# K one tile ahead of V, P.V one step late, wq in longer runs, and a LayerNorm split around a product, in a memory-bound decode kernel

## The chip, the cores and the metric

The kernel runs on one core of a Trainium2 chip (trn2). The metric is the device time of one execution in microseconds (us). Times quoted below are medians of several executions; the profile's span is one execution, from its first to its last instruction, and is 1.7 to 1.9 us shorter than the time of the same execution.

## The reference, cut to what matters

One decode step (one new token) of a pre-LayerNorm attention block with a key and value cache, followed by a pre-LayerNorm dense block:

```python
B, D, H, Sk, Dh, F = 4, 640, 32, 4096, 128, 1728            # bf16 everywhere
x = A_x                                                     # [4, 1, 640]
q = (layernorm(x) @ wq).reshape(B, 1, H, Dh)
scores = einsum("bhqd,bhkd->bhqk", q, k_cache) * Dh ** -0.5
o = einsum("bhqk,bhkd->bhqd", softmax(scores), v_cache)
h = x + o.reshape(B, 1, H * Dh) @ wo
a = layernorm(h) @ w1 + b1
out = h + (a * tanh(softplus(a))) @ w2
```

The caches are 4 x 32 x 4096 x 128 values each, 134 MB for K and 134 MB for V. Each byte is used once. wq, wo, w1 and w2 together are 15 MB.

## The kernel before: the parts that matter

The caches pass through four SBUF slots of 32 KB per partition ("stream"). A tile is 4 heads of one batch row, 4.19 MB, each partition getting one contiguous row of 32 KB. There are 32 K tiles and 32 V tiles, called k0 to k31 and v0 to v31 here. All loads are issued in order on one queue; a load waits until its slot's former tile has been read.

```python
stream = ctx.enter_context(tc.tile_pool(name="stream", bufs=NSLOT))      # 4 slots

for c in range(DC):                                   # wq: 5 loads of 1 MB, 8 KB runs
    if c % WQC == 0:
        wq_t.append(stream.tile([P, SLOT], BF16, tag="s", name=f"wq{c}"))
    nc.sync.dma_start(out=wq_t[-1][:, (c % WQC) * H * Dh : (c % WQC + 1) * H * Dh],
                      in_=A_wq[c * P : (c + 1) * P, :])
# ...
for i in range(NT - 1):                               # k0 v0 k1 v1 ... k30 k31 v30 v31
    loads.append((load_cache, kt, A_k_cache, i, "k"))
    if i == NT - 2:
        loads.append((load_cache, kt, A_k_cache, NT - 1, "k"))
    loads.append((load_cache, vt, A_v_cache, i, "v"))
loads.append((load_cache, vt, A_v_cache, NT - 1, "v", 4))                # in 4 quarters
loads.append((load_wo_late,))                         # wo (second half), then w1, w2
# ...
loads.append((load_mlp,))
```

For each tile VectorE multiplies K by the query (four multiplies of 2.28 us), TensorE folds the products, VectorE and ScalarE make the exponentials, and TensorE multiplies them with V (P.V).

```python
for i in range(NT):
    issue_loads(i + LA)
    for s in range(NSUB):                             # scores of tile i
        emit_mult(i, s)
        # ... emit_scores, emit_mask, emit_fold
    # ...
    if i < last - 1:
        for s in range(NSUB):
            emit_pv(i, s)                             # P.V of the same tile
        emit_pv_copy(i)
# ... P.V of the last two tiles, wo product into y_ps
```

Behind the attention, LayerNorm is finished before the w1 product starts:

```python
s_ps = ones_d.T @ [y, y*y]                            # (sketch) sums over partitions
# mean, variance, sqrt (ScalarE), reciprocal, (y - mean) * rstd -> ln2 (bf16)
h1_ps = ident.T @ b1T                                 # (sketch) bias first
# 70 matmuls of 4 columns: h1_ps += w1 tile x ln2; exp; mish; 56 matmuls with w2
```

The softmax here doesn't subtract the row's maximum and nothing guards it: scores larger than these inputs give would overflow.

## Time and profile before

| | before |
|---|---|
| median of 3 runs | 676.73 us (676.01 to 677.57) |
| span of the profiled execution | 673.0 us |
| moved | 283.81 MB |
| VectorE / TensorE busy | 61% / 64% |

The first view is from the page of the kernel before: the busy tenths of the 16 DMA engines and what they moved, each in 40 slices of 16.8 us, and the packets.

```profile
DMA  9999999999999999999999999999999999999993
GB/s 368 425 428 434 442 427 422 432 434 439 428 424 432 433 437 428 425 429 435 433 430 428 429 429 435 428 432 433 432 429 430 431 429 433 430 430 433 414 415 160
DMA packets 13015, 283.81 MB, mean 422 GB/s; under 512 B 1652, under 2 KB 1720, under 8 KB 3768
```

The loads never pause.

The second view is the timeline of the end: start, duration, engine, line, operation, output and inputs, and in brackets the idle time and what ended it. `k_3601` is k30, `k_3603` is k31, `v_3705` is v31.

```profile
619.31 4.49 DVE L283 TENSOR_TENSOR prod<-k_3601,qbc 128x4096 bf16<-128x4096 bf16 x2 [5.12 <-DMA k_3601<-in_A_k_cache_dram]
...
634.42 4.49 DVE L283 TENSOR_TENSOR prod<-k_3603,qbc 128x4096 bf16<-128x4096 bf16 x2
...
653.36 1.04 PE L351 MATMUL pv_124<-v_3705,e 128*16 128x512 bf16 x16
...
658.68 0.18 DVE L468 COPY st<-y_ps 128x20 f32<-128x20 f32 x1 [0.87 <-PE y_ps L408]
...
661.22 4.74 PE L522 MATMUL h_ps<-ln_4048,w_slot 128*64 128x4 bf16 x70 [1.39 <-DVE ln_4048 L502]
...
669.84 0.32 DVE L571 CAST o_bf<-y_ps 128x160 bf16<-128x160 f32 x1 [2.24 <-PE y_ps L565]
```

The first multiply of k30 waits for its load, that of k31 does not: it follows k30's. The last P.V, w1 and w2 products wait for no load either. From 619.3 on the end is compute.

The third view is the windows of the same stretch: start and end in us, length, then for PE (TensorE matmuls), PEld (weight loads), DVE (VectorE), ACT (ScalarE) and POOL the busy time and the count of instructions, then the granted TensorE clock (1.00 is full speed), the DMA share and GB/s.

```profile
656.00:658.00 2.00, 2.00 (x80) 2.00 (x80) 0.37 (x2) 0.00 (x0) 0.00 (x0) 0.97 1.03 423
658.00:660.00 2.00, 1.34 (x28) 1.21 (x25) 0.71 (x4) 1.09 (x2) 0.00 (x0) 0.50 1.02 417
660.00:662.00 2.00, 0.78 (x13) 0.76 (x13) 0.79 (x6) 1.92 (x3) 0.00 (x0) 0.50 0.69 282
662.00:664.00 2.00, 2.00 (x34) 1.97 (x33) 0.00 (x0) 0.04 (x1) 0.00 (x0) 0.50 0.47 188
664.00:666.00 2.00, 2.00 (x31) 1.87 (x30) 0.00 (x0) 0.01 (x1) 0.00 (x0) 0.50 0.14 58
```

The loads run at full rate until 660 and fade out until almost 666 (w2 is the last). The granted clock is 0.50 from 658 on.

### The profile page before, as it was taken

The page shows a single profiled execution, that of the slowest core. Times are in us where ns is not written, and L with a number is a line of the kernel's source. Part 1 is how long each engine was busy: PE and PEld are TensorE (multiplying, and loading weights), DVE is VectorE, ACT ScalarE, POOL GpSimd, SP SyncE. Part 2 cuts the span into 40 slices and gives each one's busy share as a digit, 9 for nine tenths or more (in the row PEclk, how much of TensorE's full clock was granted, in tenths as well). Part 3 has the DMA queues.
Part 4 walks back from the last instruction along what each step waited for, and adds up shares of the span by engine and source line. Part 5 has one row for each costly group of instructions (what it writes and reads, how often), then busy time and mean ns, then how long its engine had stood idle before and what let it go on. Part 6 is the DMA issues. An engine that isn't in the chain of part 4 may idle for free.

```text
span 673.0 us, 6966 instructions
## 1 busy us (share of the span) xinstructions
PE 431.2 (64%) x2933; PEld 192.9 (29%) x2933; DVE 410.7 (61%) x474; ACT 75.4 (11%) x312; POOL 1.9 (0%) x9
## 2 busy tenths in 40 slices
PE   1947765755767745776566667476557766655776
PEld 0313322322323312332223323222223322222335
DVE  3455665755658746576555767585565766576842
ACT  0401100111101101010000110011010100001011
POOL 1000000000000000000000000000000000000000
PEclk9979767889868878896687987787788967788895
DMA  9999999999999999999999999999999999999993
GB/s 368 425 428 434 442 427 422 432 434 439 428 424 432 433 437 428 425 429 435 433 430 428 429 429 435 428 432 433 432 429 430 431 429 433 430 430 433 414 415 160
DMA packets 13015, 283.81 MB, mean 422 GB/s; under 512 B 1652, under 2 KB 1720, under 8 KB 3768
## 3 DMA queue, kind: packets, MB, share of 16 engines
q1 hardware_dynamic: 12656, 283.27, 98.3%
q8 instruction: 23, 0.38, 0.2%
q10 hardware_dynamic: 328, 0.09, 0.1%
q14 instruction: 8, 0.07, 0.0%
HBM read 283.35 MB, written 0.01 MB: 421 GB/s over the span
## 4 chain that ended last, share of the span: by engine, by line
DMA 59%; DVE 19%; PE 19%; issue 1%; ACT 0%; SPq 0%; DVEq 0%; ACTq 0%
DVE prod L283 16%; PE red L295 14%; DMA k_342<-in_A_k_cache_dram 4%; DMA k_1516<-in_A_k_cache_dram 4%; DMA k_1041<-in_A_k_cache_dram 4%; DMA k_1991<-in_A_k_cache_dram 4%; DMA k_566<-in_A_k_cache_dram 4%; DMA k_2464<-in_A_k_cache_dram 4%; DMA k_3370<-in_A_k_cache_dram 4%; DMA k_2917<-in_A_k_cache_dram 4%; DMA k_3148<-in_A_k_cache_dram 4%; DMA k_1767<-in_A_k_cache_dram 4%; DMA k_817<-in_A_k_cache_dram 3%; DMA k_2695<-in_A_k_cache_dram 3%; DMA k_3601<-in_A_k_cache_dram 3%; DMA k_1292<-in_A_k_cache_dram 3%
## 5 line engine op out<-in xcount | busy, mean ns | idle before, releaser
L295 PE MATMUL red<-prod,ident 128*128 128x512 bf16 x1024 | 302.3, 454 | 218.7 <-DVE prod L283 217.7
L295 PEld LDWEIGHTS <-ident 128*128 128x128 bf16 x1024 | 116.5, 115 | 386.1 <-issue 319.7
L312 DVE TENSOR_REDUCE s_f<-red 128x32 f32<-128x512 f32 x128 | 88.0, 688 | 79.3 <-PE red L295 79.2
L315 ACT ACTIVATE ex<-s_f 128x32 bf16<-128x32 f32 x128 | 29.4, 229 | 518.0 <-DVE s_f L312 518.0
L322 DVE TENSOR_TENSOR e<-ex,hmask 128x128 bf16<-128x128 bf16 x128 | 36.4, 284 | 6.1 <-ACT ex L315 6.1
L372 PEld LDWEIGHTS o_ps<-selo,pv_sb 128*128 128x128 f32 x256 | 33.4, 191 | 6.0 <-ACT pv_sb L362 1.7
L351 PEld LDWEIGHTS <-e 128*16 128x16 bf16 x1024 | 18.4, 88 | 45.8 <-DVE e L322 21.8
L372 PE MATMUL o_ps<-selo,pv_sb 128*128 128x4 f32 x256 | 30.6, 243 | 0.7 <-ACT pv_sb L362 0.7
L315 ACT ACTIVATION_READ_ACCUMULATOR ex<-s_f 128x1 f32 x128 | 23.8, 186 | 0.0
L283 DVE TENSOR_TENSOR prod<-k_82,qbc 128x4096 bf16<-128x4096 bf16 x4 | 9.1, 2286 | 17.9 <-DMA k_82<-in_A_k_cache_dram 17.9
L378 DVE TENSOR_TENSOR OT<-o_ps,rl 128x16 bf16<-128x16 f32 x8 | 1.6, 195 | 21.7 <-PE o_ps L372 21.7
L255 PE MATMUL q_ps<-wq_74,lnT 128*4 128x512 bf16 x32 | 10.9, 463 | 4.1 <-DMA wq_74<-in_A_wq_dram 4.1
L283 DVE TENSOR_TENSOR prod<-k_244,qbc 128x4096 bf16<-128x4096 bf16 x4 | 9.1, 2286 | 6.7 <-DMA k_244<-in_A_k_cache_dram 6.7
L283 DVE TENSOR_TENSOR prod<-k_1415,qbc 128x4096 bf16<-128x4096 bf16 x4 | 9.1, 2285 | 6.7 <-DMA k_1415<-in_A_k_cache_dram 6.7
L283 DVE TENSOR_TENSOR prod<-k_3148,qbc 128x4096 bf16<-128x4096 bf16 x4 | 9.1, 2285 | 6.3 <-DMA k_3148<-in_A_k_cache_dram 6.3
L283 DVE TENSOR_TENSOR prod<-k_940,qbc 128x4096 bf16<-128x4096 bf16 x4 | 9.1, 2287 | 6.1 <-DMA k_940<-in_A_k_cache_dram 6.1
L283 DVE TENSOR_TENSOR prod<-k_1767,qbc 128x4096 bf16<-128x4096 bf16 x4 | 9.1, 2285 | 5.9 <-DMA k_1767<-in_A_k_cache_dram 5.9
L283 DVE TENSOR_TENSOR prod<-k_1890,qbc 128x4096 bf16<-128x4096 bf16 x4 | 9.1, 2287 | 5.7 <-DMA k_1890<-in_A_k_cache_dram 5.7
L283 DVE TENSOR_TENSOR prod<-k_465,qbc 128x4096 bf16<-128x4096 bf16 x4 | 9.1, 2286 | 5.7 <-DMA k_465<-in_A_k_cache_dram 5.7
L283 DVE TENSOR_TENSOR prod<-k_2363,qbc 128x4096 bf16<-128x4096 bf16 x4 | 9.1, 2285 | 5.6 <-DMA k_2363<-in_A_k_cache_dram 5.6
L283 DVE TENSOR_TENSOR prod<-k_2695,qbc 128x4096 bf16<-128x4096 bf16 x4 | 9.1, 2286 | 5.1 <-DMA k_2695<-in_A_k_cache_dram 5.1
L283 DVE TENSOR_TENSOR prod<-k_3601,qbc 128x4096 bf16<-128x4096 bf16 x4 | 9.1, 2284 | 5.1 <-DMA k_3601<-in_A_k_cache_dram 5.1
(175 smaller groups left out, 377.9 us busy)
## 6 DMA issues: line engine op xcount, KB each, us to landing
wq_74<-in_A_wq_dram SPq DMA_DIRECT2D x4, 1024.0 KB, 9.7
k_82<-in_A_k_cache_dram SPq DMA_DIRECT2D x1, 4096.0 KB, 20.5
v_84<-in_A_v_cache_dram SPq DMA_DIRECT2D x1, 4096.0 KB
k_244<-in_A_k_cache_dram SPq DMA_DIRECT2D x1, 4096.0 KB
v_246<-in_A_v_cache_dram SPq DMA_DIRECT2D x1, 4096.0 KB
k_342<-in_A_k_cache_dram SPq DMA_DIRECT2D x1, 4096.0 KB
v_344<-in_A_v_cache_dram SPq DMA_DIRECT2D x1, 4096.0 KB, 35.1
k_465<-in_A_k_cache_dram SPq DMA_DIRECT2D x1, 4096.0 KB
```

The source lines that it names most:

```text
L255: nc.tensor.matmul(q_ps[:, :], lhsT=lnT[:, c, :], rhs=wq_t[c // WQC][:, o : o + 512], start=(c == 0), stop=(c == DC - 1),)
L283: nc.vector.tensor_tensor(out=t[:, :, :], in0=kt[i][:, s * RS : (s + 1) * RS, :], in1=q_bc[hg][:, b, :].unsqueeze(1).to_broadcast([P, RS, ...
L295: nc.tensor.matmul(red[:, :, :], lhsT=ident[:, :], rhs=t[:, :, c * CW : (c + 1) * CW], start=(c == 0), stop=(c == Dh // CW - 1),)
L312: nc.vector.tensor_reduce(out=s_t[i][:, sl], in_=reds.pop((i, s))[:, :, :], axis=AX.X, op=ALU.add)
L315: nc.scalar.activation(out=ex_t[i][:, sl], in_=s_t[i][:, sl], func=ACT.Exp, scale=SCALE, accum_out=rs_t[hg][:, b, s : s + 1],)
L322: nc.vector.tensor_tensor(out=e_t[i][:, sl, :], in0=ex_t[i][:, sl].unsqueeze(2).to_broadcast([P, RS, G]), in1=hmask[:, :].unsqueeze(1).to_ ...
L351: nc.tensor.matmul(pvs[i % 2][k * QD : k * QD + RQ * G, :], lhsT=e_t[i][:, u * RQ : (u + 1) * RQ, :], rhs=vt[i][:, u * RQ : (u + 1) * RQ, ...
L372: nc.tensor.matmul(o_ps[hg][:, b, :], lhsT=t[:, r, :], rhs=selo[:, r, :], start=(r == 0), stop=(r == RQ - 1),)
L378: nc.vector.tensor_tensor(out=OT[:, hg * G : (hg + 1) * G, :].rearrange("p g b -> p b g"), in0=o_ps.pop(hg)[:, :, :], in1=rl.pop(hg)[:, :] ...
```

## The change

Its intent: let the last K tile arrive before its scores are needed and the last P.V wait for nothing but V; load wq in fewer, longer runs; and start the w1 product as soon as the mean is known, with the square root and 1/std behind it (the bias is multiplied by std so that it comes out right).

```diff
-    for c in range(DC):
-        if c % WQC == 0:
-            wq_t.append(stream.tile([P, SLOT], BF16, tag="s", name=f"wq{c}"))
+    wq_v = A_wq.rearrange("(p c) n -> p (c n)", c=DC)
+    for c0 in range(0, DC, WQC):
+        n = min(WQC, DC - c0) * H * Dh
+        wq_t.append(stream.tile([P, SLOT], BF16, tag="s", name=f"wq{c0}"))
         nc.sync.dma_start(
-            out=wq_t[-1][:, (c % WQC) * H * Dh : (c % WQC + 1) * H * Dh],
-            in_=A_wq[c * P : (c + 1) * P, :],
+            out=wq_t[-1][:, 0:n], in_=wq_v[:, c0 * H * Dh : c0 * H * Dh + n]
         )
# ...
-    for i in range(NT - 1):
+    for i in range(NT):
         loads.append((load_cache, kt, A_k_cache, i, "k"))
-        if i == NT - 2:
-            loads.append((load_cache, kt, A_k_cache, NT - 1, "k"))
-        loads.append((load_cache, vt, A_v_cache, i, "v"))
+        if i > 0:
+            loads.append((load_cache, vt, A_v_cache, i - 1, "v"))
# ... w2_tail's load moves from the head to behind tile 0
+    ident_f = consts.tile([P, P], FP32)
+    nc.vector.tensor_copy(out=ident_f[:, :], in_=ident[:, :])
# ... 
-        if i < last - 1:
+        if i > 0:
             for s in range(NSUB):
-                emit_pv(i, s)
-            emit_pv_copy(i)
+                emit_pv(i - 1, s)
+            emit_pv_copy(i - 1)
# ... w1 product: rhs=ln2 becomes rhs=cen (mean taken off, bf16); the bias follows by
+            nc.tensor.matmul(
+                h1_ps[:, :, :], lhsT=ident_f[:, :], rhs=b1s[:, :, :], start=False, stop=False
+            )
# ... and behind the product
+    h1 = consts.tile([P, FC, N], FP32)
+    nc.vector.tensor_tensor(
+        out=h1[:, :, :], in0=h1_ps[:, :, :],
+        in1=rstd[:, :].unsqueeze(1).to_broadcast([P, FC, N]), op=ALU.mult,
+    )
```

More of the change, by code (lines that the diff above doesn't have):

```diff
@@ L158 @@
     )
-    nc.scalar.dma_start(out=w2_tail[0:FT, :], in_=B_w2[FM * P : F, :])
     ident = consts.tile([P, P], BF16)
@@ L228, with transposed @@
     )
-    def transposed(rows, dst):
+    def transposed(rows, dst, split):
         tp = ps.tile([P, DC * N], FP32, tag="misc", name="tp")
@@ L234, in transposed @@
                 tp[:, c * N : (c + 1) * N],
-                lhsT=rows[0:N, c * P : (c + 1) * P], rhs=ident[0:N, 0:N],
+                lhsT=split(rows)[:, c, :], rhs=ident[0:N, 0:N],
                 start=True, stop=True,
@@ L241 @@
     xT = consts.tile([P, DC, N], BF16)
-    transposed(ln1, lnT[:, :, :])
-    transposed(x_bf, xT[:, :, :])
+    transposed(ln1, lnT[:, :, :], lambda t: t[:, :].rearrange("n (p c) -> n c p", c=DC))
+    transposed(x_bf, xT[:, :, :], lambda t: t[:, :].rearrange("n (c p) -> n c p", c=DC))
     nc.vector.tensor_copy(
@@ L429 @@
             emit_fold(i, s)
-            if i > 0 and s == 1 and i < last:
-                emit_o(i - 1)
-                if b == 0:
+            if i > 1 and s == 1:
+                emit_o(i - 2)
+                if b == 1:
                     emit_ot(hg - 1)
-            if b == 0 and i > 0 and s == 2:
+            if hg > 0 and b == 1 and s == 2:
                 emit_perm(hg - 1)
-            if b == 0 and i > 0 and s == 3 and hg <= WLATE:
+            if hg > 0 and b == 1 and s == 3 and hg <= WLATE:
                 emit_wo(hg - 1)
@@ L440 @@
         emit_mask(i, NSUB - 1)
-        if i < last - 1:
+        if i == 0:
+            nc.scalar.dma_start(out=w2_tail[0:FT, :], in_=B_w2[FM * P : F, :])
+            nc.scalar.dma_start(
+                out=w2_tail[FT : FT + CG, :], in_=B_w2[F - CG : F, :]
+            )
+        if i > 0:
             for s in range(NSUB):
-                emit_pv(i, s)
-            emit_pv_copy(i)
+                emit_pv(i - 1, s)
+            emit_pv_copy(i - 1)
         if b == N - 1:
@@ L448 @@
             emit_qbc(hg + 1)
-    for s in range(NSUB):
-        emit_pv(last - 1, s)
-    emit_pv_copy(last - 1)
     emit_pv(last, 0)
@@ L464 @@
     emit_wo(WLATE + 3)
+    FC = FM + 1
+    h1_ps = ps.tile([P, FC, N], FP32, tag="red", name="h1_ps")
+    nc.tensor.matmul(
+        h1_ps[:, :, :], lhsT=zeros[:, :], rhs=zeros[:, 0 : FC * N], start=True, stop=False
+    )
     st = consts.tile([P, 2, DC, N], FP32)
@@ L469, with emit_mean @@
     nc.scalar.activation(out=st[:, 1, :, :], in_=y_ps[:, :, :], func=ACT.Square)
-    s_ps = ps.tile([P, 2 * DC * N], FP32, tag="misc", name="s_ps")
-    nc.tensor.matmul(
-        s_ps[:, :], lhsT=ones_d[:, :], rhs=st[:, :, :, :].rearrange("p k c n -> p (k c n)"),
-        start=True, stop=True,
-    )
+    s_ps = []
+    for k in range(2):
+        t = ps.tile([P, DC * N], FP32, tag="misc", name="s_ps")
+        nc.tensor.matmul(
+            t[:, :], lhsT=ones_d[:, :], rhs=st[:, k, :, :].rearrange("p c n -> p (c n)"),
+            start=True, stop=True,
+        )
+        s_ps.append(t)
+    mu = consts.tile([P, 2, N], FP32)
+    def emit_mean(k):
+        nc.vector.tensor_reduce(
+            out=mu[:, k, :], in_=s_ps[k][:, :].rearrange("p (c n) -> p n c", c=DC),
+            axis=AX.X, op=ALU.add,
+        )
+    emit_mean(0)
+    cen = consts.tile([P, DC, N], BF16)
+    nc.vector.tensor_tensor(
+        out=cen[:, :, :], in0=st[:, 0, :, :],
+        in1=mu[:, 0, :].unsqueeze(1).to_broadcast([P, DC, N]), op=ALU.subtract,
+    )
+    emit_mean(1)
+    msq = consts.tile([P, N], FP32)
+    nc.vector.tensor_tensor(out=msq[:, :], in0=mu[:, 0, :], in1=mu[:, 0, :], op=ALU.mult)
+    var = consts.tile([P, N], FP32)
+    nc.vector.tensor_tensor(out=var[:, :], in0=mu[:, 1, :], in1=msq[:, :], op=ALU.subtract)
+    std2 = consts.tile([P, N], FP32)
+    nc.scalar.activation(
+        out=std2[:, :], in_=var[:, :], func=ACT.Sqrt, bias=eps4[:, :], scale=1.0
+    )
+    b1s = consts.tile([P, FC, N], FP32)
+    nc.vector.tensor_tensor(
+        out=b1s[:, :, :], in0=b1T[:, :].unsqueeze(2).to_broadcast([P, FC, N]),
+        in1=std2[:, :].unsqueeze(1).to_broadcast([P, FC, N]), op=ALU.mult,
+    )
+    rstd = consts.tile([P, N], FP32)
+    nc.vector.reciprocal(out=rstd[:, :], in_=std2[:, :])
     h_hi = consts.tile([P, DC, N], BF16)
@@ L480 @@
     )
-    mu = consts.tile([P, 2, N], FP32)
-    nc.vector.tensor_reduce(
-        out=mu[:, :, :],
-        in_=s_ps[:, :].rearrange("p (k c n) -> p k n c", k=2, c=DC),
-        axis=AX.X, op=ALU.add,
-    )
-    msq = consts.tile([P, N], FP32)
-    nc.vector.tensor_tensor(out=msq[:, :], in0=mu[:, 0, :], in1=mu[:, 0, :], op=ALU.mult)
-    var = consts.tile([P, N], FP32)
-    nc.vector.tensor_tensor(out=var[:, :], in0=mu[:, 1, :], in1=msq[:, :], op=ALU.subtract)
-    rstd = consts.tile([P, N], FP32)
-    nc.scalar.activation(
-        out=rstd[:, :], in_=var[:, :], func=ACT.Sqrt, bias=eps4[:, :], scale=1.0
-    )
-    cen = consts.tile([P, DC, N], FP32)
-    nc.vector.tensor_tensor(
-        out=cen[:, :, :], in0=st[:, 0, :, :],
-        in1=mu[:, 0, :].unsqueeze(1).to_broadcast([P, DC, N]), op=ALU.subtract,
-    )
-    nc.vector.reciprocal(out=rstd[:, :], in_=rstd[:, :])
-    ln2 = consts.tile([P, DC, N], BF16)
-    nc.vector.tensor_tensor(
-        out=ln2[:, :, :], in0=cen[:, :, :],
-        in1=rstd[:, :].unsqueeze(1).to_broadcast([P, DC, N]), op=ALU.mult,
-    )
-    FC = FM + 1
-    w1_sb = mlp_w["w1"]
-    h1_ps = ps.tile([P, FC, N], FP32, tag="red", name="h1_ps")
-    nc.tensor.matmul(
-        h1_ps[:, :, :], lhsT=ident[:, :],
-        rhs=b1T[:, :].unsqueeze(2).to_broadcast([P, FC, N]), start=True, stop=False,
-    )
+    w1_sb = mlp_w["w1"]
     for c0, c1 in zip(W1S, W1S[1:]):
+        if c1 == DC:
+            nc.tensor.matmul(
+                h1_ps[:, :, :], lhsT=ident_f[:, :], rhs=b1s[:, :, :], start=False, stop=False
+            )
         for j in [FM] + list(range(FM)):
@@ L522 @@
                 nc.tensor.matmul(
-                    h1_ps[0 : (P if j < FM else FT), j, :], lhsT=w, rhs=ln2[:, c, :],
+                    h1_ps[0 : (P if j < FM else FT), j, :], lhsT=w, rhs=cen[:, c, :],
                     start=False, stop=(c == DC - 1 and j == FM - 1),
@@ L546 @@
     hm2 = consts.tile([P, FC, N], FP32)
-    nc.scalar.activation(out=ta[:, :, :], in_=h1_ps[:, :, :], func=ACT.Exp, scale=1.0)
-    nc.vector.tensor_scalar_mul(out=hm2[:, :, :], in0=h1_ps[:, :, :], scalar1=-2.0)
+    h1 = consts.tile([P, FC, N], FP32)
+    nc.vector.tensor_tensor(
+        out=h1[:, :, :], in0=h1_ps[:, :, :],
+        in1=rstd[:, :].unsqueeze(1).to_broadcast([P, FC, N]), op=ALU.mult,
+    )
+    nc.scalar.activation(out=ta[:, :, :], in_=h1[:, :, :], func=ACT.Exp, scale=1.0)
+    nc.vector.tensor_scalar_mul(out=hm2[:, :, :], in0=h1[:, :, :], scalar1=-2.0)
     nc.vector.scalar_tensor_tensor(
```

## The prediction

> **What bounds the kernel now.** The DMA stream. The page shows 283.81 MB moved, DMA 9 in 39 of 40 slices, and 422 to 442 GB/s in slices 2 to 37 (mean about 430). The Trainium skill, "DMA: Bandwidth & Descriptors", "Where 436 GB/s comes from", puts the fabric ceiling at 435 GB/s; this trace agrees with it within about 1%. Reordering cache loads cannot speed the middle. DVE (61%) and PE (64%) finish a tile in about 15 us (k30 landed at 619.3, next multiply at 634.4; timeline) where two cache tiles take 19.4 us to arrive. Only head and tail can move.
>
> **Tail before** (timeline, windows, issue times plus landing times). k30 lands at 619.3 and k31, by my estimate, at 629.2 (4.19 MB at 425 GB/s), but k31's multiply starts at 634.4 because k30 is still being scored: 5.2 us lost. Scores end at 649.0, last P.V at 654.4, wo product 658.7, first w1 matmul 661.2, w1 done 665.9, act at 667.6, w2 done 669.8, end 673.0. Loads meanwhile: the last v quarter about 648.6, w1 660.5, last piece of w2 about 665.6 (issued 651.8, 13.8 us to landing). So compute ends about 2 us behind the last load.
>
> **What the change does.**
> - k30 moves from 61st to 60th cache tile, so it lands near 609.6, and k31 no longer waits behind it: its multiply starts at 629.2 when it lands. Scores end about 644 (-5). P.V of tile 31 then waits for v31 (648.6) and ends about 649.3 (-5).
> - But wo comes behind v31: its last quarter lands about 654.9 (2.62 MB at 415 GB/s), so y is done about 655.5 to 656.3 (-2.5 to -3).
> - The mean alone ahead of w1: before, y to w1 took 2.57 us with a 1.28 us table load, square root and reciprocal in it. After: about 1.5 us (-1). Added: a float32 bias matmul (about 0.3, mostly hidden) and one 128x56 multiply by 1/std (about 0.25) behind w1.
> - w1's 70 matmuls took 4.74 us, 68 ns each, at a granted clock of 0.50 (windows 658 to 672), which I expect to stay. The Trainium skill, "TensorE: Matmul & The Clock Gate", "Part 1", names 4/8 as the cold state; the trace agrees (0.50). They also wait for w1's last piece at 660.1 to 660.5. w1 done about 662 to 663, act about 664.5.
> - w2's last piece still lands about 665.5, unmoved. w2 done 666 to 667.1, output 3.2 us later: 669.3 to 670.4 against 673.0.
>
> **Head.** wq as one 32 KB-run load: its five pieces landed 2.5 us apart (419 GB/s; 430 would save 0.3 us). k0 follows behind (26.2), so 0 to 0.4 us.
>
> **Sum.** -2.6 to -3.7 in the tail, 0 to -0.4 in the head: about -3.3 us, 0.5%. 676.7 becomes 673.4 us; range 670.6 to 676.2. Faster by over 2%: 0.01; within 2%: 0.98; slower: 0.01.
>
> **What would show it.** Slices of the middle unchanged near 430 GB/s; last k multiply about 5 us earlier and released by its own DMA; P.V of the last tile released by DMA v; wo and w1 products with DMA waits; no square root between y and the first w1 matmul.
>
> **What would make it wrong.** A change of the mean DMA rate by 0.5% from the new order is 3 us, as large as the gain. A stall in the load queue (late slot release of v29 or k31). A last w2 landing that moves. The clock falling to 0.50 already during the wo product (gives back about 1.5 us).

## The result, and the profile after

The kernel after took 669.51 us (669.23 to 669.87, 4 runs) against 676.89 us for the kernel before (676.01 to 677.57, 4 runs): 7.4 us less. A ratio is the mean time of one kernel's runs over that of the other's of the same rounds, so it is not quite the ratio of these medians: 0.9892, 95% interval 0.9875 to 0.9909. That is inside 2%, as forecast, but below the stated range of 670.6 to 676.2, and 2.2 times the predicted gain. The two profiled executions differ by less, 673.0 against 667.5 us of span: the profiled one of the kernel before took 674.76 us and was faster than the others of its kernel here.

The page of the kernel after, same lines as before:

```profile
DMA  9999999999999999999999999999999999999995
GB/s 376 440 411 438 419 438 435 432 427 439 432 427 430 430 436 429 438 437 423 432 437 431 433 428 436 437 430 427 434 437 436 429 429 432 438 431 430 427 415 241
DMA packets 12591, 283.81 MB, mean 425 GB/s; under 512 B 1608, under 2 KB 1680, under 8 KB 3728
```

The timeline of the end of the kernel after (`k_3545` is k31, `v_3666` is v31):

```profile
627.02 4.50 DVE L284 TENSOR_TENSOR prod<-k_3545,qbc 128x4096 bf16<-128x4096 bf16 x2 [4.92 <-DMA k_3545<-in_A_k_cache_dram]
...
646.49 0.61 PE L352 MATMUL pv_124<-v_3666,e 128*16 128x512 bf16 x8 [1.04 <-DMA v_3666<-in_A_v_cache_dram]
...
653.39 0.18 DVE L477 COPY st<-y_ps 128x20 f32<-128x20 f32 x1 [2.29 <-PE y_ps L409]
...
656.90 1.89 PE L537 MATMUL h_ps<-cen,w_slot 128*64 128x4 bf16 x28 [0.20 <-DMA w_slot<-in_B_w_dram]
...
664.37 0.33 DVE L591 CAST o_bf<-y_ps 128x160 bf16<-128x160 f32 x1 [2.24 <-PE y_ps L585]
```

And its windows:

```profile
648.00:650.00 2.00, 2.00 (x37) 2.00 (x38) 0.19 (x1) 0.00 (x0) 0.00 (x0) 0.56 1.02 420
...
656.00:658.00 2.00, 1.80 (x29) 1.70 (x29) 0.09 (x1) 0.78 (x1) 0.00 (x0) 0.50 1.01 407
658.00:660.00 2.00, 2.00 (x27) 1.88 (x27) 0.00 (x0) 0.00 (x0) 0.00 (x0) 0.50 0.70 291
660.00:662.00 2.00, 1.12 (x23) 0.63 (x21) 1.41 (x6) 0.25 (x1) 0.00 (x0) 0.50 0.47 196
662.00:664.00 2.00, 1.82 (x56) 1.65 (x56) 0.13 (x1) 0.00 (x0) 0.00 (x0) 0.50 0.09 31
```

The mechanism that was forecast is there: k31 is now released by its own load, the last quarter of P.V by v31, the middle of the w1 product by w1. But every one of these loads came 2 to 3 us earlier than forecast: k31 at 627.0 instead of 629.2, and the stream fades out at 658 instead of 660. The same bytes, and the stream ended earlier.

To see the stream itself I read the completion counts that the trace keeps. The Trainium skill ("DMA: Bandwidth & Descriptors", "Why a DMA increments its semaphore by 16 and not by 1") says that a DMA's semaphore gets one increment from each of the engines that it runs on. These traces agree: a cache load shows 16 increments. So the first of the sixteen tells when the fastest engine was done, the last tells the slowest. In the kernel before the fastest engine lands a tile every 9.713 us (mean of 46 pairs of neighbouring tiles), in the kernel after every 9.684 us, evenly from 60 us to the end. And w2, the last load, is complete at 665.5 before and at 662.96 after.

So the question was what made a stream faster that moves the same bytes to the same slots: the order, wq's longer runs, w2's moved rows, or chance.

### The profile page after: what moved, and what is told of

It reads as the page before. It is cut to its first block, busy times and chain, and to the rows that moved or that the text cites. A ratio compares the mean times of both kernels' runs of the same rounds, so it can differ in the third digit from the quotient of the medians. Undisturbed runs are those within 1.5% of the kernel's fastest.

```text
span 667.5 us, 6967 instructions
## 1 busy us (share of the span) xinstructions
PE 426.0 (64%) x2937; PEld 198.2 (30%) x2937; DVE 411.7 (62%) x477; ACT 75.5 (11%) x312; POOL 1.9 (0%) x9
## 4 chain that ended last, share of the span: by engine, by line
DMA 61%; DVE 19%; PE 18%; issue 1%; ACT 0%; SPq 0%; DVEq 0%; ACTq 0%
DVE prod L284 16%; PE red L296 14%; DMA k_1005<-in_A_k_cache_dram 4%; DMA k_530<-in_A_k_cache_dram 4%; DMA k_1480<-in_A_k_cache_dram 4%; DMA k_1955<-in_A_k_cache_dram 4%; DMA k_2881<-in_A_k_cache_dram 4%; DMA k_2428<-in_A_k_cache_dram 4%; DMA k_3334<-in_A_k_cache_dram 4%; DMA k_1691<-in_A_k_cache_dram 4%; DMA k_310<-in_A_k_cache_dram 4%; DMA k_3092<-in_A_k_cache_dram 4%; DMA k_1216<-in_A_k_cache_dram 3%; DMA k_741<-in_A_k_cache_dram 3%; DMA v_3666<-in_A_v_cache_dram 3%; DMA k_2166<-in_A_k_cache_dram 3%
## 5 line engine op out<-in xcount | busy, mean ns | idle before, releaser
L352 PEld LDWEIGHTS <-e 128*16 128x16 bf16 x1024 | 22.6, 89 | 36.8 <-issue 15.5
```

Source lines behind the costliest of these rows:

```text
L352: nc.tensor.matmul(pvs[i % 2][k * QD : k * QD + RQ * G, :], lhsT=e_t[i][:, u * RQ : (u + 1) * RQ, :], rhs=vt[i][:, u * RQ : (u + 1) * RQ, ...
```

## The experiments

Each "before" time below is of runs on the same chip. In those the kernel before had medians of 675.2 to 676.5 us, while the expectations count from 676.9: what is compared with them is the difference, not the time itself.

**e1: the kernel before again**, no edit, for a second trace.

> The kernel before, unchanged, for a second trace of it. In the first trace the fastest DMA engine finished the last v quarter 618.2 us after k0, the slowest 4.8 us behind the fastest, and the span was 673.0 us, 2 us shorter than the timed runs suggest. Theory P (the load stream itself became faster by the change): this trace shows the same 618 us or more, against 617.1 in the trace after. Rival N (the 1 to 2 us by which the stream ran ahead in the trace after is a difference between executions): this trace lies anywhere in 616.5 to 619.5.

Measured: 675.44 us, ratio 0.9999 (0.9974 to 1.0024). The fastest engine lands a tile every 9.714 us and finishes the last v quarter 618.5 us after k0, as theory P has it; w2 is complete at 666.0. The pace is not a difference between executions. The other 15 traces confirm it: each kernel has one of two paces, and none lies between.

**e2: the load order and the late P.V alone**, on the kernel before.

```diff
-    for i in range(NT - 1):
+    for i in range(NT):
         loads.append((load_cache, kt, A_k_cache, i, "k"))
-        if i == NT - 2:
-            loads.append((load_cache, kt, A_k_cache, NT - 1, "k"))
-        loads.append((load_cache, vt, A_v_cache, i, "v"))
+        if i > 0:
+            loads.append((load_cache, vt, A_v_cache, i - 1, "v"))
# ... and emit_pv(i - 1, s), emit_o(i - 2) as in the change
```

> Kernel before with the load order and the delayed P.V alone. Theory T (tail: k31 no longer waits behind k30's scoring, the last P.V waits for v31, wo comes right behind): about 3 us of the 7.4 us, so 673.5 to 674.5. Theory P-order (the order also speeds the stream): 5 us or more, 671 to 672. If the gain needs the w1 part too, because w1 waits for the LayerNorm either way: 1 to 2 us, 675.

Measured: 671.94 us (671.77 to 672.69), ratio 0.9950 (0.9928 to 0.9972): 3.5 us. Its pace is 9.715 us and w2 is complete at 665.5, as before. (The time itself lies in the range of theory P-order, but the kernel before took 675.39 in this call and not 676.9; the gain of 3.5 is that of theory T, and the pace excludes P-order.) So the order gives what the prediction gave to the whole change, and does not touch the stream. The waits are those forecast, within 0.2 us of the forecast times (629.2 for k31, 649.3 for the end of P.V):

```profile
629.21 4.49 DVE L282 TENSOR_TENSOR prod<-k,qbc 128x4096 bf16<-128x4096 bf16 x2 [2.47 <-DMA k<-in_A_k_cache_dram]
...
648.81 0.67 PE L350 MATMUL pv<-v,e 128*16 128x512 bf16 x8 [1.72 <-DMA v<-in_A_v_cache_dram]
```

**e3: wq in 32 KB runs alone**, on the kernel before.

```diff
-    for c in range(DC):          # five loads of 1 MB, 8 KB runs
+    for c0 in range(0, DC, WQC): # one load of 4 MB with 32 KB runs, one of 1 MB
```

> Kernel before with wq in 32 KB runs alone (and the matching transposed rows). Prediction: 0 to 0.4 us faster, 676.5 to 677. Theory P-wq (fewer, longer packets at the head leave the 16 engines in a better step for the whole run): 2 us or more faster, about 674.5, although its tail is compute-bound, because k30 lands earlier by the same amount.

Measured: 675.14 us, ratio 0.9999 (0.9975 to 1.0022), pace 9.713. Nothing.

**e4: the kernel after with wq as before.**

> Kernel after with wq back in 8 KB runs. Prediction: 669.5 to 670. Theory P-wq: 671.5 or more, with k31 landing 2 us later than 627.0 in its trace.

Measured: 669.44 us (668.82 to 669.95), pace 9.679. Nothing, again. wq's form is worth less than can be seen here.

**e5: the kernel after with the order of before.**

> Kernel after with the load order and P.V timing of before. Theory T: loses what the order gives, 3 us or more, 672.5 to 674; k31's first multiply waits again for k30's scores. Theory P-order: 675 or more. If the wq part carried the stream gain: 671.5 to 673.

Measured: 674.33 us, but scattered from 672.36 to 675.45; pace 9.683. Without the order 4.8 us are lost, more than e2 gained with it (the sum below comes back to this). This kernel has the faster pace, which again frees the order from having caused it.

**e6: the kernel after with the LayerNorm of before.**

```diff
-    # w1 product on (y - mean), std on the bias, 1/std behind
+    # sqrt, reciprocal and scaling ahead of the w1 product, as in the kernel before
-    ident_f = consts.tile([P, P], FP32)
```

> Kernel after with the LayerNorm in front of w1 as before. Prediction: the w1 product then starts about 1 us later and, as w1 lands late anyway, ends at most 1 us later: 670 to 671. If the w1 part is hidden behind w1's landing: 669.5, no change.

Measured: 672.37 us (671.91 to 672.78): 2.9 us slower than the kernel after, more than either of the two cases that I had expected, and its pace is the slow one, 9.712; w2 is complete at 666.1.

**e7: the split LayerNorm alone**, on the kernel before.

> Kernel before with the split LayerNorm alone. In the kernel before the tail is compute-bound from k30 on, w1's last piece lands at 660.5 and w1 starts at 661.2, so about 1 us earlier start is limited by that landing: gain 0.5 to 1 us, 676.

Measured: 671.62 us (669.74 to 674.59), ratio 0.9939 (0.9915 to 0.9963). I had expected 0.5 to 1 us and got about 4. And the pace is the fast one, 9.681: a k tile in the middle of the run lands earlier because of an edit of the last 15 us. No instruction of the LayerNorm runs then. One thing that an edit of the end can change for the whole run is where things lie in memory, and that can be tested.

**e8: the kernel after with w2's 64 rows loaded at the head.**

> Kernel after with the 64 rows of w2 loaded at the head again. Prediction: no difference within 0.3 us (80 KB is 0.2 us of the stream wherever it goes). Rival: small packets at the head delay the first wq packets and put some engines behind: 0.5 to 1 us slower.

Measured: 669.58 us, pace 9.680. Nothing.

The built programs tell where the four stream slots begin in each partition. In the kernel before the first begins at byte 56704, which is 128 modulo 256; in the kernel after at byte 57600, which is 0 modulo 256, because the new constants lie ahead of the slots and take 896 bytes more. The slots are 32 KB each, so all four have the same remainder. All kernels with the split LayerNorm had 0, all with the old one had 128. The Trainium skill ("DMA: Bandwidth & Descriptors", "How a descriptor splits into AXI transactions") says that a descriptor (one contiguous run of bytes, here a row of 32 KB) is cut at 256-byte boundaries and that one which doesn't start on such a boundary pays for the bytes ahead of its start. That gave theory A: it is the address. The rival S: something else of the split LayerNorm does it. The next four kernels move the address by making one small constant longer, which moves everything behind it, the slots included, and changes no instruction.

```diff
-    eps4 = consts.tile([P, 1], FP32)
-    nc.vector.memset(eps4[:, :], EPS)
+    eps4 = consts.tile([P, 40], FP32)          # 128 bytes longer; only column 0 is used
+    nc.vector.memset(eps4[:, 0:1], EPS)
```

**f1: the kernel before, 128 bytes further** (slots at 0 modulo 256).

> Kernel before with one constant tile made 128 bytes longer and nothing else: the four stream slots move from byte 56704 (128 modulo 256) to 56832 (0 modulo 256) of each partition. Theory A (a cache row that starts on a 256-byte boundary in SBUF moves faster): the fastest engine lands a tile every 9.68 us instead of 9.71, k30 lands near 617.5 instead of 619.3 to 620.1, the time falls by 2 to 3 us to about 673. Rival S (the new LayerNorm makes it faster in some other way, such as its float32 matmul or the instruction stream): no change, 675.5.

Measured: 673.61 us (671.53 to 675.10), ratio 0.9973 (0.9951 to 0.9995): 1.6 us faster by the medians, less than the 2 to 3 us expected. The pace (9.676) is as theory A has it, and the trace shows k30 2.2 us earlier than in the kernel before:

```profile
617.16 4.50 DVE L283 TENSOR_TENSOR prod<-k,qbc 128x4096 bf16<-128x4096 bf16 x2 [2.60 <-DMA k<-in_A_k_cache_dram]
```

**f2: the kernel after, 128 bytes further** (slots at 128 modulo 256).

> Kernel after with the same constant 128 bytes longer: slots at 57728, 128 modulo 256. Theory A: the pace falls back to 9.71 us a tile, wo, w1 and w2 land 2.5 to 3 us later, time 672 to 672.5. Rival S: unchanged, 669.5.

Measured: 672.66 us (672.41 to 672.97), ratio 0.9957 (0.9942 to 0.9971); pace 9.714. Three us of the gain are gone with 128 unused bytes. Its timeline has the same waits as the kernel after, each later:

```profile
630.12 4.49 DVE L284 TENSOR_TENSOR prod<-k,qbc 128x4096 bf16<-128x4096 bf16 x2 [2.45 <-DMA k<-in_A_k_cache_dram]
...
649.76 0.98 PE L352 MATMUL pv<-v,e 128*16 128x512 bf16 x8 [1.49 <-DMA v<-in_A_v_cache_dram]
...
656.77 0.18 DVE L477 COPY st<-y_ps 128x20 f32<-128x20 f32 x1 [1.73 <-PE y_ps L409]
...
660.25 1.92 PE L537 MATMUL h_ps<-cen,w_slot 128*64 128x4 bf16 x28 [0.18 <-DMA w_slot<-in_B_w_dram]
...
667.77 0.32 DVE L591 CAST o_bf<-y_ps 128x160 bf16<-128x160 f32 x1 [2.24 <-PE y_ps L585]
```

These are close to the prediction's own figures, 0.5 to 1.5 us later: it had k31 at 629.2, the last P.V done at 649.3 (here 650.7), y at 655.5 to 656.3, the end at 669.3 to 670.4 (here 670.9). f2 is, nearly, the kernel that was predicted.

**f3: the kernel after with the old LayerNorm, but aligned.**

> Kernel after with the old LayerNorm, but slots at 56832 (0 modulo 256). Run without that alignment (e6) it took 672.4. Theory A: 669.5 to 670.2, so that the split LayerNorm itself is worth at most 0.7 us. Rival S: 672.4 again.

Measured: 669.74 us (669.47 to 670.28), ratio 0.9914 (0.9899 to 0.9929); pace 9.683. With the address held, taking the split LayerNorm out costs 0.2 us, which is within the scatter. And f2, off the boundary, took 672.66: 2.9 us for the address. The timeline shows the same waits as in the kernel after, at nearly the same times:

```profile
627.37 4.49 DVE L282 TENSOR_TENSOR prod<-k,qbc 128x4096 bf16<-128x4096 bf16 x2 [4.91 <-DMA k<-in_A_k_cache_dram]
...
646.80 0.61 PE L350 MATMUL pv<-v,e 128*16 128x512 bf16 x8 [0.99 <-DMA v<-in_A_v_cache_dram]
...
664.89 0.32 DVE L573 CAST o_bf<-y_ps 128x160 bf16<-128x160 f32 x1 [2.24 <-PE y_ps L567]
```

**f4: the kernel before with the split LayerNorm, misaligned.**

> Kernel before with the split LayerNorm, but slots at 57728 (128 modulo 256). Aligned by chance (e7) it took 671.6. Theory A: 674.5 to 675.2, 0.5 to 1 us under before. Rival S: 671.6 again.

Measured: 675.76 us, ratio 0.9999 (0.9980 to 1.0018); pace 9.717. The 4 us of e7 are gone. Nothing is left of the LayerNorm's own gain, less than I had expected. One thing stays open: e7 and f1 have the same remainder and the old order, yet e7 gained 4.1 us and f1 1.6. e5, which has the split LayerNorm too, gained 1.4. The old order's scatter, below, is of that size, and no run separates the two.

**g1: the kernel after, 64 bytes further** (slots at 64 modulo 256).

> Kernel after with the stream slots at byte 57664, 64 modulo 256. If any start off a 256-byte boundary costs the same (one more piece for each 32 KB row): 9.71 us a tile as in f2, 672 to 673. If only the offset of 128, or a 32- or 64-byte boundary, matters: 669.5.

Measured: 672.29 us (672.05 to 672.61), pace 9.718, against 669.50 for g3 on the same chip: 2.8 us. The offset of 64 cost about what the one of 128 cost in f2 (3.1 us).

**g2: the kernel after with empty matmuls in TensorE's waits**, to keep its clock up. The Trainium skill ("TensorE: Matmul & The Clock Gate", "Part 1") says that the clock is gated by how busy TensorE has been over some 3.4 us; no run here measures that length.

```diff
+    def warm(n):
+        for _ in range(n):
+            nc.tensor.matmul(pvs[(last - 1) % 2][:, :], lhsT=zeros[:, :],
+                             rhs=vt[last][:, 0:RQ, :], start=True, stop=True,
+                             skip_group_check=True)
# 3 behind the third and 3 behind the fourth P.V part, 2 inside the wo product,
# 3 behind the sums of y, 3 behind the first part of the w1 product
```

> Kernel after with 14 empty 128x512 matmuls put where TensorE waits in the tail, into an accumulator that has been read already, to keep the granted clock at 1.0 from 648 on. If the half clock is on the chain: the w1 product ends near 659, act 0.8 to 1.3 us earlier, and the end is set by w2's landing at 663.0: 668.3 to 669 against g3. If the empty matmuls do not hold the clock, or delay the real ones: 669.5 to 671.

Measured: 671.59 us (671.24 to 672.36), 2.1 us slower than g3 and above both ranges that I had expected. The windows of g2:

```profile
648.00:650.00 2.00, 1.84 (x30) 1.46 (x28) 0.19 (x1) 0.24 (x1) 0.00 (x0) 1.00 1.00 411
650.00:652.00 2.00, 1.46 (x51) 1.38 (x52) 0.17 (x1) 0.00 (x0) 0.00 (x0) 0.90 1.02 422
652.00:654.00 2.00, 1.67 (x33) 0.89 (x31) 0.12 (x1) 0.00 (x0) 0.00 (x0) 0.50 1.03 421
```

and of its reference g3:

```profile
648.00:650.00 2.00, 1.65 (x8) 1.65 (x9) 0.00 (x0) 0.30 (x1) 0.00 (x0) 0.50 1.02 421
650.00:652.00 2.00, 2.00 (x71) 1.99 (x71) 0.37 (x2) 0.00 (x0) 0.00 (x0) 0.50 1.00 413
```

The clock was held up for about 4 us longer than in g3, through the stretch that waits for wo anyway, and then fell all the same. From there the empty matmuls ran at the half clock in front of real ones:

```profile
654.99 1.45 PE L457 MATMUL pv<-v,zeros 128*128 128x512 bf16 x3
...
658.53 1.06 PE L457 MATMUL pv<-v,zeros 128*128 128x512 bf16 x2 [0.24 <-issue]
```

The first w1 matmul came at 656.37 instead of g3's 655.34, the last ended at 662.96 instead of 660.86. Whether a denser filling would hold the clock and pay for itself is left open.

**g3: the kernel after again.**

> Kernel after, unchanged, as the reference of g1 and g2 on the same chip: 669.2 to 670 with slots at 0 modulo 256, 9.68 us a tile.

Measured: 669.50 us (669.15 to 669.95), ratio 0.9900 (0.9882 to 0.9918), pace 9.680.

The stream in all 17 traces, from the completion counts (fastest engine's mean time per tile; the moment at which w2, the last load, was complete):

| slots modulo 256 | traces | us per tile, fastest engine | w2 complete, us |
|---|---|---|---|
| 128 or 64 | before, e1, e2, e3, e6, f2, f4, g1 | 9.712 to 9.718 | 665.5 to 666.3 |
| 0 | after, e4, e5, e7, e8, f1, f3, g2, g3 | 9.676 to 9.684 | 662.6 to 663.6 |

The two groups don't overlap, whatever the order, the LayerNorm or wq's form. The two addresses of the fast group, 57600 and 56832, are 256 and 0 modulo 512, so a 512-byte boundary is not needed.

The trace also keeps how long each DMA packet took, and a row of 32 KB is one packet. In the nine traces of the fast group 98 to 99% of these packets took 1213 ns. In the eight others only 10 to 31% did; the median was 1215 or 1216 ns, and most of the rest lay between 1214 and 1224. The mean difference, leaving out the few packets above 1240 ns, is about 3.5 ns, or by estimate some 1.8 us over the 504 such rows that each engine moves. So it is the rows into the slots that got slower. Of the tiles that loads write, the padding moves only the slots and the four tiles of the first half of wo. These start at 0 modulo 256 in the kernel before and at 128 in the kernel after, and their rows of 5 KB show no such cost: 483 of 512 packets took 196 ns before, 507 of 512 after. (In g1, where they start at 192, 132 of 512 did.) So a remainder of 128 did not cost every load, and what in the hardware makes the slots' rows slower stays open.

**The scatter of the old order.** Kernels with the old order scatter by some 4 us (the kernel before: 673.6 to 678.1), those with the new order mostly stay within 1 us; e8 had one run at 672.72. The profiled execution of e3 was the longest of its six (677.7 us). In its windows the granted clock falls just where the last P.V products stand:

```profile
650.00:652.00 2.00, 1.40 (x14) 0.72 (x18) 0.77 (x4) 0.00 (x0) 0.00 (x0) 0.76 1.02 413
652.00:654.00 2.00, 2.00 (x24) 0.79 (x20) 0.00 (x0) 0.00 (x0) 0.00 (x0) 0.50 1.02 416
```

The last P.V then ended 7.1 us after the scores instead of 5.4 in the kernel before, where the clock was 1.00 in these windows:

```profile
650.00:652.00 2.00, 2.00 (x44) 0.89 (x36) 0.04 (x1) 0.37 (x1) 0.00 (x0) 1.00 1.03 419
652.00:654.00 2.00, 2.00 (x32) 1.27 (x24) 0.00 (x0) 0.22 (x1) 0.00 (x0) 1.00 1.03 414
```

f4's trace shows the same loss (7.0 us). With the old order the end is a chain of compute, so such a loss goes into the time; with the new order the chain waits for loads. This is read from traces; no experiment tested it.

## Why the prediction was wrong

- *What bounds the kernel*: right. The DMA stream did, and all of the gain is in when loads land and in what waits for them.
- *"Reordering cache loads cannot speed the middle"*: right. e2 has the new order and the old pace, e5 the old order and the new pace. The prediction named a change of the DMA rate "from the new order" first among what would make it wrong; the rate did change, but the order was not why.
- *k31 no longer waits behind k30, P.V waits for v31, wo right behind; -2.6 to -3.7 in the tail*: right, in mechanism and nearly in size. The order alone gave 3.5 us (e2), with the waits at the predicted times; f2, the whole change at the old pace, took 2.6 us less than the kernel before of its call (675.22), where 3.3 were predicted.
- *The w1 product can start 1 us earlier but waits for w1; bias and 1/std cost a little*: right that little comes of it. Held at the same address it is worth 0.2 us with the new order (after against f3), -0.3 us off the boundary (f2 against e6, on another chip), and nothing that could be measured with the old order (f4). The start of the w1 product does come earlier (1.40 us behind y instead of 2.54), but the product waits for w1's load, then does the float32 bias matmul (0.66 us, where 0.3 was forecast) and the extra multiply (0.22 us).
- *Head, 0 to -0.4 us from wq*: right; e3 and e4 show nothing.
- *The clock falling to 0.50 already during the wo product*: it did (0.56 in 648 to 650 of the trace after). Holding it up did not pay in the one way tried (g2).
- **The step that failed:** *"w2's last piece still lands about 665.5, unmoved"*, and with it "slices of the middle unchanged near 430 GB/s" (slices 2 to 37 of the two pages have means of 430.8 and 431.9, too close to show it). The stream became 0.35% faster (9.680 against 9.714 us a tile), and w2 was complete 2.7 us earlier on the mean (662.6 to 663.6 against 665.5 to 666.3). The cause is the start address of the stream slots, moved onto a 256-byte boundary by the constants of the new LayerNorm. Shown by f1, f2 and g1, in which unused bytes alone switch the pace, and by f3, which keeps it without the LayerNorm. The padding moves all tiles that lie behind it, not the slots alone; that it is the slots follows from the packets, since those that got slower go there. Why they take longer is not shown.

The sum: 3.5 us for the order (e2) and 2.8 us (g1 against g3) to 3.1 us (f2 against after) for the address make 6.3 to 6.6 of the 7.4 us. The rest lies within the scatter of the kernel before, whose medians differ by 1.7 us. The two parts do not simply add: in the one call that has all four kernels, the address is worth 1.6 us with the old order (before 675.22, f1 673.61) and 2.9 us with the new (f2 672.66, f3 669.74), and the order 2.6 us at the old address and 3.9 us at the new. With the old order the end is bound by compute, so an earlier landing helps less there. (f2 has the split LayerNorm and f3 has not.)

No tried version beats the kernel after by more than the scatter. f3 equals it within 0.3 us with the simpler LayerNorm.

## What to carry to other kernels

In a kernel whose time is a load stream at its ceiling, look at the byte address at which the streamed tiles begin. Here an edit of constants somewhere else moved it onto a 256-byte boundary, and a stream faster by 0.35% gave 2.8 to 3.1 us, nearly as much as a well-planned reordering of its end (3.5 us). When an edit changes something at a time at which none of its instructions run, compare the memory layouts before believing its intent, and test with a few unused bytes. At the end of such a stream, order the loads so that compute waits for the last of them rather than for each other; that gave 3.5 us, as planned.

## What the Trainium skill lacked or had wrong

- "DMA: Bandwidth & Descriptors", "How a descriptor splits into AXI transactions" shows the 256-byte rule only on descriptors of 96 and 576 bytes, and speaks of reads. These runs show that the start on the SBUF side of a load counts, and its cost for 32 KB rows: 9.714 against 9.680 us a tile, 0.35%; the kernel's time differed by 2.8 us of 670 (g1). Counting beats as the page does gives an estimate of 1028 instead of 1024 for an offset of 128 bytes (0.39%) and 1026 for one of 64 (0.20%); measured were 0.35% (f2) and 0.39% (g1), so for 64 the count falls short. Nor does it fit the 5 KB rows into the wo tiles, which took 196 ns from a start at 128 as from one at 0.
- The same page's "Rules for kernel authors" has no line on the alignment of the SBUF tile; here 128 unused bytes changed the time by 3.1 us (672.66 against 669.51).
- The same page, "Where 436 GB/s comes from", gives 435 GB/s as the ceiling. The fastest engine's pace is 433.3 GB/s aligned and 431.8 misaligned (4.194 MB over 9.680 and 9.714 us), so these traces agree within 1%.
- No page gives a figure for how far engines drift apart in a long stream on the sync queue. Here the slowest engine finishes each load 4.2 to 5.5 us behind the fastest by 600 us, which fits the 5 us over which the stream fades out; the gap grows in steps (by 1.5 us near 525 us in the trace after, where the profile has a 16 KB instruction packet at 524.7). That the packets cause the steps was not tested, and others (at 489.4 and 546.3) brought no step.
- "TensorE: Matmul & The Clock Gate", "Part 1" ties the clock to how busy TensorE is. In the trace before the clock fell from 0.97 to 0.50 directly behind a window in which TensorE was busy for 2.00 of 2 us with matmuls of 4 columns, and in g2 14 empty matmuls of 512 columns spread over 14 us (the trace has 11 of them) held it up for only about 4 us longer. The page doesn't say how much such short matmuls count.
